# Up projection of a two-stage kernel: the low part of x's last 64 rows in row-half matmuls, and 256 columns everywhere

## The chip, the cores and the metric

The kernel runs on one core of a Trainium2 chip. The metric is the device time of one execution in microseconds; the median of three runs of the kernel before is 454.5 us (454.33 to 455.55).

## What is computed

Two stages. The first is a gated linear attention (an mLSTM cell) over 4 sequences of 768 steps with 8 heads of 40, the second a feed-forward layer on its output x of 3072 tokens by 320:

```python
h = x @ w_in                                                # 320 -> 2048
sp = np.maximum(h, 0.0) + np.log1p(np.exp(-np.abs(h)))
g = h * erf(sp)
return (g @ w_out).astype(np.float32)                       # 2048 -> 320
```

The weights come as float64 and are decoded on the chip.

## The kernel before, in words

The sequence is cut into 12 chunks of 64 steps, so a chunk has 256 tokens. `attention(c)` makes the chunk's attention on TensorE in many small matmuls of 40 or 64 rows: line 509 the scores, 518 the state times the queries, 523 the new state, 531 (536 in the first three chunks) the heads. Line 389 turns the output on TensorE to put features on rows; lines 392 and 393 do this for the last 64 features in the first three chunks, once for either half of 128 rows. Lines 402 and 406 split the turned x into a high part `xh` (rounded to TensorE's short format, fp32r) and the rest `xl`. x has 320 features, so both have three slices of rows: 128, 128, and 64 rows that are there twice, in rows 0 to 63 and again in rows 64 to 127.

w_in is split likewise into `wh` and `wl`, but the 64 rows of its third slice hold both: in `wh[:, 2]` one half of the 128 rows is the high part and the other half the low part, which `weights_tail` arranges (ScalarE line 694 writes the high part to the rows where the decoded word lies, VectorE line 698 the low part to the other half). One matmul with `x[:, 2]`, which is there twice, thus multiplies high and low part of w_in at once.

`mlp(g)` is the feed-forward layer for one chunk k and a quarter q of the 2048 features, 48 blocks in all. Its up projection writes `h` in four groups of 128 features by 256 tokens. For g below 16 (line 759, two steps of 16 matmuls of 256 columns) every group has eight matmuls: three for each full slice (wh x, wh xl, wl x) and two for the third (wh x, wh xl). From g = 16 on (`wide`, four steps of 5 matmuls) x and xl lie side by side as 512 columns, so a group is three matmuls of 512 columns and two of 256, and the sums with x and with xl land in two halves of a PSUM bank. ScalarE copies `h` to `hb` (line 770); for the wide form it copies one half and VectorE adds the other (line 775). `h` has two banks that all steps take in turn. Then come softplus, erf, a product (lines 779 to 787), a split into `gh` and `gl` (797 to 803) and the down projection on TensorE into `pob` (lines 823 to 828, 320 columns), as four steps a block: for each half of the tokens a long one with `gh` and a short one with `gl`.

The order of the work is a list written out in the file, `ORDER`: each entry is a step, and every engine's instructions stand in the order of the steps. Each step has a cost in microseconds beside it that only the search for the list uses.

Of the kernel before, what the change touches and what calls it, by code (L numbers as in the profile page):

```python
# [9 lines left out]
F32 = mybir.dt.float32  # L10
# [23 lines left out]
class Plan:  # L34
# [136 lines left out]
def tile_mlstm_moe(  # L171
# [503 lines left out]
    def weights_tail(i):  # L675
# [4 lines left out]
        def _():  # L680
            raw = new('raw', [128, 1024], R, I32)
            for j in range(2):
                part = 2 * i + j
                nc.sync.dma_start(raw[64 * j:64 * j + 64], w_in.bitcast(I32)[256:320, part * 1024:(part + 1) * 1024])
# [264 lines left out]
```

## Time and profile before

| | |
|---|---|
| median of three runs | 454.5 us |
| profiled execution | 455.36 us |
| its span, first to last instruction | 453.6 us |
| TensorE busy | 441.3 us (97%) |
| VectorE busy | 356.9 us (79%) |
| ScalarE busy | 328.1 us (72%) |
| DMA, HBM traffic | 46.77 MB read, 4.13 MB written |
| TensorE clock granted | 0.999 of full (2.4 GHz) |

Busy shares tell which engine could be the bound; the waits of that engine tell whether it is. Matmuls are pipelined, so the pitch of a run of matmuls is read from the differences of their starts, not from their durations.

### The profile page before, as it was taken

What the parts mean: (1) busy time and instruction counts of PE and PEld (TensorE: products, weight loads), DVE (VectorE), ACT (ScalarE), POOL (GpSimd) and SP (SyncE); (2) the same over time, 40 slices, a digit from 0 to 9 for tenths busy, and PEclk for the clock granted to TensorE, in tenths of its full rate; (3) what the DMA queues carried; (4) which work ended last, traced back from release to release, by engine and by line L of the source; (5) the groups of instructions that cost most, each with busy time, mean ns of one, the idle gap of its engine ahead of it and who ended that gap; (6) DMA issues with size and microseconds to landing.
All of it is one profiled execution on the core that took longest, in us unless ns stands there. A gap on an engine that the chain in (4) does not pass through costs nothing.

```text
span 453.6 us, 13042 instructions
## 1 busy us (share of the span) xinstructions
PE 441.3 (97%) x5542; PEld 396.2 (87%) x5542; DVE 356.9 (79%) x709; ACT 328.1 (72%) x524; POOL 39.0 (9%) x62
## 2 busy tenths in 40 slices
PE   6979999999999999999999999999999999999996
PEld 4558898897999999998998999999998899999996
DVE  4897998799779888877888869978687877665862
ACT  4766999899589987676785777765776476765850
POOL 2000051003111004002001102300000000000000
PEclk9999999999999999999999999999999999999999
DMA  7969797818834053412247114340322100000011
GB/s 257 293 173 335 226 280 223 224 48 259 222 97 127 3 117 106 106 45 87 83 131 206 49 43 124 115 128 1 108 107 85 31 1 0 14 17 17 14 30 29
DMA packets 46826, 51.74 MB, mean 114 GB/s; under 512 B 27056, under 2 KB 31664, under 8 KB 46768
## 3 DMA queue, kind: packets, MB, share of 16 engines
q1 hardware_dynamic: 46768, 50.91, 38.7%
q8 instruction: 43, 0.70, 0.6%
q14 instruction: 15, 0.12, 0.1%
HBM read 46.77 MB, written 4.13 MB: 112 GB/s over the span
## 4 chain that ended last, share of the span: by engine, by line
PE 88%; DVE 6%; DMA 3%; issue 1%; ACT 1%; SPq 1%; DVEq 0%
PE h L759 37%; PE pob L827 11%; PE pob L825 11%; PE pob L828 11%; PE pa L518 3%; PE pa L509 2%; PE pa L531 2%; PE pob L823 2%; PE pa L389 2%; PE pa L523 1%; DMA gd<-x 1%; DMA raw<-in_w_in_dram 1%; PE pob L283 1%; PE pa L446 1%; DVE wo L724 1%
## 5 line engine op out<-in xcount | busy, mean ns | idle before, releaser
L759 PE MATMUL h<-xh,wh 128*128 128x256 f32 (+1 forms) x768 | 203.4, 343 | 1.6 <-DVE xh L406 1.2
L759 PEld LDWEIGHTS h<-xh,wh 128*128 128x128 f32 x768 | 126.3, 188 | 15.6 <-DVE xh L406 1.4
L770 ACT ACTIVATE hb<-h 128x256 f32<-128x256 f32 (+1 forms) x160 | 66.2, 423 | 68.9 <-PE h L759 66.1
L759 PE MATMUL h<-xh,wl 128*128 128x256 f32 x384 | 107.9, 281 | 1.0 <-DVE wl L660 1.0
L827 PE MATMUL pob<-woh,gh 128*128 128x320 f32 x336 | 100.8, 312 | 0.0
L828 PE MATMUL pob<-wo,gh 128*128 128x320 f32 x336 | 99.9, 309 | 0.0
L775 DVE TENSOR_TENSOR hb<-h,hb 128x256 f32<-128x256 f32 x128 | 52.9, 420 | 40.9 <-ACT hb L770 40.0
L759 PEld LDWEIGHTS h<-xh,wl 128*128 128x128 f32 x384 | 72.4, 188 | 2.7 <-DVE wl L660 1.2
L887 ACT ACT_TABLE_LOAD x54 | 69.3, 1283 | 1.7 <-PEq L937 0.8
L787 DVE TENSOR_TENSOR n<-n,hb 128x1024 f32<-128x1024 f32 x48 | 59.0, 1229 | 13.4 <-ACT n L783 13.3
L828 PEld LDWEIGHTS pob<-wo,gh 128*128 128x128 f32 x336 | 63.1, 188 | 1.7
L827 PEld LDWEIGHTS pob<-woh,gh 128*128 128x128 f32 x336 | 63.2, 188 | 0.5
L825 PE MATMUL pob<-woh,gl 128*128 128x320 f32 x336 | 62.3, 311 | 0.0
L487 POOL TENSOR_SCALAR_AFFINE_SELECT dm<-dm 128x512 f32<-128x512 f32 (+1 forms) x40 | 35.6, 892 | 278.2 <-ACT dm L467 275.8
L825 PEld LDWEIGHTS pob<-woh,gl 128*128 128x128 f32 x336 | 53.8, 188 | 2.3
L803 DVE TENSOR_TENSOR gl<-n,gh 128x1024 fp32r<-128x1024 f32 x44 | 53.5, 1222 | 0.3
L779 ACT ACTIVATE n<-hb 128x1024 f32<-128x1024 f32 x48 | 49.5, 1055 | 3.0 <-DVE hb L775 1.7
L783 ACT ACTIVATE n<-n 128x1024 f32<-128x1024 f32 x48 | 50.0, 1055 | 0.2
L797 ACT ACTIVATE gh<-n 128x1024 fp32r<-128x1024 f32 x28 | 29.4, 1054 | 4.1 <-DVE n L787 2.4
L627 DVE TENSOR_TENSOR state<-state,pa 40x328 f32<-40x328 f32 (+1 forms) x36 | 17.8, 494 | 5.0 <-PE pa L531 3.3
L567 DVE TENSOR_TENSOR dm<-pa,dm 128x512 f32<-128x512 f32 x24 | 16.5, 687 | 5.7 <-PE pa L509 5.4
L833 ACT ACTIVATE o<-pob 128x320 f32<-128x320 f32 x22 | 9.4, 434 | 14.9 <-PE pob L825 14.9
(103 smaller groups left out, 481.2 us busy)
## 6 DMA issues: line engine op xcount, KB each, us to landing
qk<-in_qk_dram SPq DMA_DIRECT2D x24, 512.0 KB
kvo<-in_kvo_dram SPq DMA_DIRECT2D x24, 484.0 KB
eT<-gd SPq DMA_DIRECT2D x44, 128.0 KB
raw<-in_w_out_dram SPq DMA_DIRECT2D x16, 320.0 KB
dm<-gd SPq DMA_DIRECT2D x40, 128.0 KB
raw<-in_w_in_dram SPq DMA_DIRECT2D x8, 512.0 KB
out_dram<-o SPq DMA_DIRECT2D x48, 80.0 KB
raw<-in_w_in_dram SPq DMA_DIRECT2D x4, 256.0 KB
```

The source lines that it names most:

```text
L487: nc.gpsimd.affine_select(out=x, in_=x, pattern=[[0, H], [1, L]], compare_op=ALU.is_ge, fill=0.0, base=base, channel_multiplier=-1)
L759: nc.tensor.matmul(h[:, n * T:n * T + n_], w, m, start=(s == 0), stop=(s == len(ops) - 1))
L770: nc.scalar.activation(part(), G(f'h{i}')[:, T:2 * T] if wide else G(f'h{i}'), AF.Copy)
L775: nc.vector.tensor_tensor(part(), G(f'h{i}')[:, 0:T], part(), op=ALU.add)
L779: nc.scalar.activation(new('n0', [128, 1024], ('n0', g)), G('hb'), AF.Softplus)
L783: nc.scalar.activation(G('n0'), G('n0'), AF.Erf)
L787: nc.vector.tensor_tensor(G('n0'), G('n0'), G('hb'), op=ALU.mult)
L803: nc.vector.tensor_tensor(new('gl', [128, 1024], ('gl', g), F32R), G('n0'), G('gh').bitcast(F32), op=ALU.subtract)
L825: nc.tensor.matmul(acc(b), G('gl')[:, ts], woh[:, j], start=False, stop=(j == NFF - 1))
L827: nc.tensor.matmul(acc(b), G('gh')[:, ts], woh[:, j], start=(j == 0), stop=False)
L828: nc.tensor.matmul(acc(b), G('gh')[:, ts], t['wol', j], start=False, stop=False)
L887: plan.run(ORDER, lambda k: nc.scalar.preload_act_table_set(KIND[k]), stay)
```

## The change

From g = 8 on (`TAILS`), the up projection gets a step of its own ahead of the rest: four matmuls of 64 rows by 256 columns, high part of w_in's last 64 rows times `xl`. Two of the four lie on rows 0 to 63 and write bank `h0`, two on rows 64 to 127 and write `h1`, in turn. The product of the two low parts of these rows falls away. The other two steps have 14 matmuls of 256 columns, two groups of seven each, and add to what the new step has begun; the wide form with its addition on VectorE is gone. The blocks below 8 keep two steps of 16.

```diff
-        wide = g >= 16
-        ups = 4 if wide else 2
+        tails = g >= TAILS
+        ends = [('wh', 2, q)]
...
+        if tails:
+            @op('PE', 0.25, mm=4, r=[(('xl', k), b) for b in range(2)] + ends, w=[(('h0', g), 't'), (('h1', g), 't')],
+                tile_=[('h', ('h0', g)), ('h', ('h1', g))], kind='m', name=f'up{g}')
+            def _():
+                h = [new('h', [128, 512], (f'h{i}', g)) for i in range(2)]
+                xr = t['xl', k]
+                for n in range(2):
+                    for i in range(2):
+                        rows, fs = slice(64 * i, 64 * i + 64), slice((4 * q + 2 * i + n) * 128, (4 * q + 2 * i + n + 1) * 128)
+                        nc.tensor.matmul(h[i][:, n * T:(n + 1) * T], wh[rows, 2, fs], xr[rows, 2], start=(n == 0), stop=False)
...
-                    if wide:
-                        ops = [(wh[:, 0, fs], both[:, 0]), (wl[:, 0, fs], x[:, 0]), (wh[:, 1, fs], both[:, 1]),
-                               (wl[:, 1, fs], x[:, 1]), (wh[:, 2, fs], both[:, 2])]
...
+                    ops = [(wh[:, 0, fs], x[:, 0]), (wh[:, 0, fs], xr[:, 0]), (wl[:, 0, fs], x[:, 0]),
+                           (wh[:, 1, fs], x[:, 1]), (wh[:, 1, fs], xr[:, 1]), (wl[:, 1, fs], x[:, 1]),
+                           (wh[:, 2, fs], x[:, 2])] + ([] if tails else [(wh[:, 2, fs], xr[:, 2])])
...
-            if wide:
-                @op('DVE', 0.33, r=[((f'h{i}', g), 0)], w=[(('hb', g), i)])
-                def _(i=i, part=part):
-                    nc.vector.tensor_tensor(part(), G(f'h{i}')[:, 0:T], part(), op=ALU.add)
```

So that the high part lies on rows 0 to 63 for the first two groups of a quarter and on rows 64 to 127 for the other two, `weights_tail` loads and splits in pieces of 256 features instead of 512, two ScalarE and two VectorE instructions where there was one of each; the loads keep their number and bytes, in runs of 2 KB instead of 4.

```diff
-                part = 2 * i + j
-                nc.sync.dma_start(raw[64 * j:64 * j + 64], w_in.bitcast(I32)[256:320, part * 1024:(part + 1) * 1024])
+                nc.sync.dma_start(raw[64 * j:64 * j + 64].rearrange("p (a w) -> p a w", a=2), src[:, :, j])
...
+                for j in range(2):
+                    nc.scalar.activation(wh[rows[j], 2, cs[j]], word(j), AF.Copy)
...
+                for j in range(2):
+                    nc.vector.tensor_tensor(wh[rows[1 - j], 2, cs[j]], word(j), wh.bitcast(F32)[rows[j], 2, cs[j]], op=ALU.subtract)
```

The list `ORDER` is another from entry 340 on. Read against the steps, it places the 40 new steps so: 20 stand between two steps of 128-row matmuls, 19 follow directly on an attention step that ends in 64-row matmuls (scores or heads) and go over to 128-row matmuls, and one follows on 128-row matmuls and is followed by such an attention step. Between the last up step of a block and the new step of the next there is always some down projection or attention.

## Rows read from the trace of the kernel before

**Rows 1.** The page: busy time by engine; TensorE's digits and clock in 40 slices.

```profile
PE 441.3 (97%) x5542; PEld 396.2 (87%) x5542; DVE 356.9 (79%) x709; ACT 328.1 (72%) x524; POOL 39.0 (9%) x62
...
PE   6979999999999999999999999999999999999996
...
PEclk9999999999999999999999999999999999999999
```

**Rows 2.** Waits of TensorE over the run: us in total, times, longest us.

```profile
PE pob L283 <- DVE state L272: 3.5, 1, 3.5
PE h L759 <- DVE xh L406: 1.2, 1, 1.2
PE h L759 <- DVE wl L660: 1.0, 1, 1.0
```

**Rows 3.** The page: the chain that ended last, by engine.

```profile
PE 88%; DVE 6%; DMA 3%; issue 1%; ACT 1%; SPq 1%; DVEq 0%
```

**Rows 4.** Busy time in one stretch: length, then us (count) by engine.

```profile
200.00:220.00 20.00, 20.00 (x210) 18.25 (x209) 15.01 (x33) 13.13 (x23) 2.44 (x2) 1.00 0.25 74
```

**Rows 5.** Pieces of the chain: start us, length us, what.

```profile
63.76 2.11 PE h L759 x16
...
115.79 1.92 PE h L759 x16
...
141.72 3.83 PE h L759 x32
...
168.57 1.87 PE h L759 x10
...
303.59 1.13 PE h L759 x5
...
310.82 0.59 PE pob L825 x4
```

**Rows 6.** Timeline of TensorE around a heads block: start us, length us, what.

```profile
302.23 0.39 PE L759 MATMUL h<-xh,wh 128*128 128x512 f32 x1
302.47 0.28 PE L759 MATMUL h<-xh,wl 128*128 128x256 f32 x1
302.58 0.40 PE L759 MATMUL h<-xh,wh 128*128 128x512 f32 x1
302.92 0.68 PE L531 MATMUL pa<-kvo,dm 64*64 64x41 f32 x32
303.52 0.50 PE L759 MATMUL h<-xh,wh 128*128 128x512 f32 x1
303.86 0.28 PE L759 MATMUL h<-xh,wl 128*128 128x256 f32 x1
```

**Rows 7.** The same block: its first four matmuls, and its last one.

```profile
302.92 0.27 PE L531 MATMUL pa<-kvo,dm 64*64 64x41 f32 x4
...
303.37 0.23 PE L531 MATMUL pa<-kvo,dm 64*64 64x41 f32 x1
```

**Rows 8.** Timeline of TensorE around a column-split transpose of an early chunk.

```profile
46.47 0.27 PE L392 MATMUL pa<-ident,kvo 128*64 128x128 f32 x1
46.67 0.43 PE L393 MATMUL pa<-ident,kvo 128*64 128x128 f32 x2
47.04 0.50 PE L759 MATMUL h<-xh,wh 128*128 128x256 f32 x2
```

**Rows 9.** Groups by line and form: busy us, mean ns, idle before and its releasers.

```profile
L770 ACT ACTIVATE hb<-h 128x256 f32<-128x256 f32 x128 | 47.3, 380 | 65.1 <-PE h L759 62.3 <-issue 2.1 <-ACT hb L770 0.5
L770 ACT ACTIVATE hb<-h 128x512 f32<-128x512 f32 x32 | 18.9, 591 | 3.8 <-PE h L759 3.8
L694 ACT ACTIVATE wh<-raw 64x512 fp32r<-64x512 f32 x4 | 2.7, 670 | 1.6 <-DVE raw L646 1.5
...
L775 DVE TENSOR_TENSOR hb<-h,hb 128x256 f32<-128x256 f32 x128 | 52.9, 420 | 40.9 <-ACT hb L770 40.0
L698 DVE TENSOR_TENSOR wh<-raw,wh 64x512 fp32r<-64x512 f32 x4 | 2.7, 687 | 0.2
```

More of the change, by code (lines that the diff above doesn't have):

```diff
@@ L101 @@
     225, 162, 273, 79, 80, 81, 82, 87, 89, 274, 202, 203, 355, 371, 206, 141, 194, 142, 121, 92, 122, 275, 276, 90, 248,
[64 rows of a table removed]
[53 rows of a table added]
 ]
-PLAIN, JOIN, GH_ACT = 4, 3, 32
+PLAIN, JOIN, GH_ACT, TAILS = 4, 3, 32, 8
 @with_exitstack
@@ L582, in _ @@
                         t[n, c] = x[:, :, i]
-                    t['x', 'both', c] = x
                 heads(r)
@@ L681, in _ @@
             raw = new('raw', [128, 1024], R, I32)
+            src = w_in.bitcast(I32)[256:320, i * 2048:(i + 1) * 2048].rearrange("p (a j w) -> p a j w", a=2, j=2)
             for j in range(2):
-                part = 2 * i + j
-                nc.sync.dma_start(raw[64 * j:64 * j + 64], w_in.bitcast(I32)[256:320, part * 1024:(part + 1) * 1024])
+                nc.sync.dma_start(raw[64 * j:64 * j + 64].rearrange("p (a w) -> p a w", a=2), src[:, :, j])
         decode(R, lambda: pair(t[R]), 512, lambda: pair(t[R])[:, :, 0], ())
-        for j in range(2):
-            part = 2 * i + j
-            cs, here, there = slice(part * 512, (part + 1) * 512), slice(64 * j, 64 * j + 64), slice(64 - 64 * j, 128 - 64 * j)
-            word = lambda here=here: pair(t[R])[here, :, 0].bitcast(F32)
-            @op('ACT', 0.56, r=[(R, 1)], w=[('wt', part)])
-            def _(cs=cs, here=here, word=word):
-                nc.scalar.activation(wh[here, 2, cs], word(), AF.Copy)
-            @op('DVE', 0.62, r=[(R, 1), ('wt', part)], w=[('wh', 2, part)])
-            def _(cs=cs, here=here, there=there, word=word):
-                nc.vector.tensor_tensor(wh[there, 2, cs], word(), wh.bitcast(F32)[here, 2, cs], op=ALU.subtract)
+        for a in range(2):
+            part = 2 * i + a
+            rows = [slice(64 * j, 64 * j + 64) for j in range(2)]
+            cs = [slice(part * 512 + 256 * j, part * 512 + 256 * j + 256) for j in range(2)]
+            word = lambda j, a=a: pair(t[R])[64 * j:64 * j + 64, 256 * a:256 * a + 256, 0].bitcast(F32)
+            @op('ACT', 0.62, r=[(R, 1)], w=[('wt', part)])
+            def _(rows=rows, cs=cs, word=word):
+                for j in range(2):
+                    nc.scalar.activation(wh[rows[j], 2, cs[j]], word(j), AF.Copy)
+            @op('DVE', 0.68, r=[(R, 1), ('wt', part)], w=[('wh', 2, part)])
+            def _(rows=rows, cs=cs, word=word):
+                for j in range(2):
+                    nc.vector.tensor_tensor(wh[rows[1 - j], 2, cs[j]], word(j), wh.bitcast(F32)[rows[j], 2, cs[j]], op=ALU.subtract)
     def weights_out(j):
@@ L734, in acc @@
             return t['po', k][:, 512 * b:512 * b + DM] if k == 1 else pob[b][:, 0:DM]
-        wide = g >= 16
-        ups = 4 if wide else 2
-        whole = [(('hb', g), i) for i in range(ups)]
-        for i in range(ups):
-            @op('PE', 0.937 if wide else 1.915, mm=5 if wide else 16, r=[((n, k), b) for n in ('xh', 'xl') for b in range(2)]
-                + [(n, s, q) for n, s in (('wh', 0), ('wh', 1), ('wh', 2), ('wl', 0), ('wl', 1))],
-                w=[((f'h{i}', g), 0)], tile_=('h', (f'h{i}', g)), kind='m', name=f'up{g}')
+        tails = g >= TAILS
@@ new lines, in mlp @@
+        whole = [(('hb', g), i) for i in range(2)]
+        ends = [('wh', 2, q)]
[9 more added lines that the diff above has]
+                        nc.tensor.matmul(h[i][:, n * T:(n + 1) * T], wh[rows, 2, fs], xr[rows, 2], start=(n == 0), stop=False)
@@ L744, in _ @@
+        for i in range(2):
+            @op('PE', 1.68 if tails else 1.915, mm=14 if tails else 16, r=[((n, k), b) for n in ('xh', 'xl') for b in range(2)] + ends
+                + [(n, s, q) for n, s in (('wh', 0), ('wh', 1), ('wl', 0), ('wl', 1))] + ([((f'h{i}', g), 't')] if tails else []),
+                w=[((f'h{i}', g), 0)], tile_=() if tails else ('h', (f'h{i}', g)), kind='m', name=f'up{g}')
             def _(i=i):
-                h = new('h', [128, 512], (f'h{i}', g))
-                x, xr, both = t['xh', k], t['xl', k], t['x', 'both', k]
@@ L747, in _ @@
-                for n in range(1 if wide else 2):
-                    j = 4 * q + (i if wide else 2 * i + n)
+                h = t[f'h{i}', g] if tails else new('h', [128, 512], (f'h{i}', g))
+                x, xr = t['xh', k], t['xl', k]
+                for n in range(2):
+                    j = 4 * q + 2 * i + n
                     fs = slice(j * 128, (j + 1) * 128)
-                    if wide:
-                        ops = [(wh[:, 0, fs], both[:, 0]), (wl[:, 0, fs], x[:, 0]), (wh[:, 1, fs], both[:, 1]),
-                               (wl[:, 1, fs], x[:, 1]), (wh[:, 2, fs], both[:, 2])]
-                    else:
-                        ops = [(wh[:, 0, fs], x[:, 0]), (wh[:, 0, fs], xr[:, 0]), (wl[:, 0, fs], x[:, 0]),
-                               (wh[:, 1, fs], x[:, 1]), (wh[:, 1, fs], xr[:, 1]), (wl[:, 1, fs], x[:, 1]),
-                               (wh[:, 2, fs], x[:, 2]), (wh[:, 2, fs], xr[:, 2])]
-                    for s, (w, m) in enumerate(ops):
-                        n_ = 2 * T if len(m.shape) == 3 else T
-                        nc.tensor.matmul(h[:, n * T:n * T + n_], w, m, start=(s == 0), stop=(s == len(ops) - 1))
@@ L761, in part @@
-            def part(i=i):
-                n = 1024 // ups
-                return G('hb')[:, i * n:(i + 1) * n]
-            @op('ACT', 0.28 if wide else 0.49, r=[((f'h{i}', g), 0)], w=[(('hb', g), i)],
-                tile_=('hb', ('hb', g)) if i == 0 else ())
-            def _(i=i, part=part):
+                    ops = [(wh[:, 0, fs], x[:, 0]), (wh[:, 0, fs], xr[:, 0]), (wl[:, 0, fs], x[:, 0]),
+                           (wh[:, 1, fs], x[:, 1]), (wh[:, 1, fs], xr[:, 1]), (wl[:, 1, fs], x[:, 1]),
+                           (wh[:, 2, fs], x[:, 2])] + ([] if tails else [(wh[:, 2, fs], xr[:, 2])])
@@ L768, in _ @@
+                    for s, (w, m) in enumerate(ops):
+                        nc.tensor.matmul(h[:, n * T:(n + 1) * T], w, m, start=(s == 0 and not tails), stop=(s == len(ops) - 1 and (n == 1 or not tails)))
+            @op('ACT', 0.49, r=[((f'h{i}', g), 0)], w=[(('hb', g), i)], tile_=('hb', ('hb', g)) if i == 0 else ())
+            def _(i=i):
                 if i == 0:
                     new('hb', [128, 1024], ('hb', g))
-                nc.scalar.activation(part(), G(f'h{i}')[:, T:2 * T] if wide else G(f'h{i}'), AF.Copy)
@@ L772, in mlp @@
-            if wide:
-                @op('DVE', 0.33, r=[((f'h{i}', g), 0)], w=[(('hb', g), i)])
-                def _(i=i, part=part):
-                    nc.vector.tensor_tensor(part(), G(f'h{i}')[:, 0:T], part(), op=ALU.add)
+                nc.scalar.activation(G('hb')[:, i * 512:(i + 1) * 512], G(f'h{i}'), AF.Copy)
         @op('ACT', 0.96, r=whole, w=[(('n0', g), 0)], tile_=('n0', ('n0', g)), table='S')
```

117 rows, old and new, of the table ORDER are left out of this document.

## The prediction

> **What bounds the kernel now.** I read the page's busy shares first: TensorE is busy 441.3 of 453.6 us, and its digits are 9 in every slice from the fourth to the last but one, at full clock throughout [rows 1]. VectorE has 79% and ScalarE 72%, so they are no bound by their sum, but either could still be late at many places. The waits of TensorE decide that: over the whole run the longest wait for another engine is 3.5 us, at the very start, then come 1.2 and 1.0 in the stage that decodes the weights, and nothing else of that size [rows 2]. The chain of waits says the same (88% TensorE), and the stretch from 200 to 220 us shows TensorE at 20.00 of 20 with VectorE at 15.0 and ScalarE at 13.1 [rows 3, 4]. So from about 47 us to the end the time is the sum of TensorE's own work, in the order of the list. What VectorE and ScalarE save is worth nothing; what a matmul step costs or gives counts one to one.
>
> **Two kinds of pitch** are needed, and both are differences of starts, since durations of single matmuls overlap. A run of 128-row up matmuls of 256 columns takes 1.92 us for 16 and 3.83 for 32, so 0.12 each; ten of the wide form, two steps, take 1.87, so 0.935 a step [rows 5]. Second, a change of the array's shape. A 512-column matmul is followed 0.24 us later by the next (302.23 to 302.47), but 0.34 later by the first of the 64-row block of the attention heads: 0.10 of idle array [rows 6]. Leaving is the same: the last small matmul starts at 303.37 and the first full one 0.15 later [rows 6, 7], where the small ones come four at a time in rounds of 0.06 (32 of them from 302.92 to 303.37), so about 0.10 more. Then the first matmul in the new shape waits for its own weights: 303.52 to 303.86 is 0.34 where 0.24 is usual, 0.10 again, because nothing could load them beforehand. The chain gives the sum of the leaving side in one number: 16 up matmuls after a 64-row block take 2.11 against 1.92, five of the wide form take 1.13 against 0.935 [rows 5]. A column-split shape pays it too: the 128x64 transposed tail in the upper half starts 0.20 after its predecessor of 128 columns, and the next full matmul finds the array 0.37 after that pair's start [rows 8].
>
> **Change, part by part.**
>
> Full-array work saved. For the 32 blocks from 16 on, four steps of 0.935 = 3.74 us become 28 matmuls of 0.12, 2 x 14/16 x 1.915 = 3.35: 0.39 saved, 12.5 in all. The eight blocks 8 to 15 go from 3.83 to 3.35: 0.48 each, 3.8. Together 16.3 us. Most of the 0.39 is one 256-column matmul per 128 features; the split into 256 columns gives back a little (a 512 at 0.23 is cheaper than two at 0.12).
>
> The new step of four 64-row matmuls, 40 times. No row shows a 64-row by 128-column matmul, so it is put together. The four of one round of a head block start within 0.02 us of each other, and 32 need 0.45 us of starts: halves of the array do run side by side when they write different banks, which is what h0 and h1 are [rows 7]. So four are two rounds of 0.12 = 0.24. On top, between two full-array steps: 0.10 to enter, 0.10 for the first weights, 0.10 to leave, 0.10 for the first weights after it. 0.64. After or before a block of 64-row matmuls in the list one idle gap and one load are paid anyway, so 0.10 + 0.10 less: 0.44. The list has 20 of either sort: 12.8 + 8.8 = 21.6 us. Bounds of one step: 0.24 from below (the columns must be streamed; less is excluded), 0.88 from above (halves one after the other, 4 x 0.12, with all four gaps; the gaps around the heads block are the nearest rows, hence 0.64 [rows 6]).
>
> What the Trainium skill says bears on the 0.40 of gaps: "TensorEngine Tiling (Array Packing)", Key Properties, has it that a change of tiling mode, not of tile, makes the engine drain. By that rule the step costs what I take; the rows agree for 64x64 and 128x64, and none shows 64x128.
>
> Evacuation. The 128 additions on VectorE (52.9 us) go; ScalarE's copies go from 47.3 + 18.9 to 96 of 0.59 = 57 us [rows 9]. Both lie under TensorE and give nothing.
>
> What is queued behind the new wait. The new step needs both banks of h free, so it waits for the second copy of the block before; on TensorE's queue all later down projections stand behind it. In the list the work between a block's last up matmul and the next new step is never under 0.86 us and in 37 of 39 cases 1.1 or more, counted with 0.59 for a short down step, twice that for a long one and 0.6 or more for an attention step [rows 5, 6]; the copy needs 0.28 for the last matmul's end and 0.59 for itself [rows 6, 9]. So at most a handful of short waits; I take 0, bound 0 to 4 us (eight of 0.5).
>
> Weight tails. Each of four splits becomes two instructions per engine: 0.67 on ScalarE and 0.69 on VectorE now. By the 128-row copies, two of 256 columns cost 2 x 0.38 - 0.59 = 0.17 more, and two additions 2 x 0.42 - 0.69 = 0.15 more [rows 9]. Only in the decode stage, where TensorE waited 1.2 and 1.0 us for such results [rows 2], can this show: bounds 0 and 4 x 0.32 = 1.3; I take 0.2. The four loads on SP's queue keep number and bytes, in pieces half as long; they are covered by the other weights still in flight, and uncovered they could cost no more than the 1.0 above.
>
> The list. It cannot win anything of TensorE's own sum; before, no wait was left in it to remove after 47 us, and the number of 64-row blocks entered from the full shape stays 44. So 0.
>
> Sum: -16.3 + 21.6 + 0.2 = +5.5 us. The profiled execution took 455.36 with a span of 453.6; on it 460.9. It stood 0.86 over the median 454.5, against which I forecast **460.0**.
>
> **Rivals.**
>
> 1, the other side: the shape change is not paid for row halves. The weights of a half are loaded while the full array still streams, and the full array's next weights behind the halves; then a step costs its 0.24, 40 of them 9.6, and the sum is -16.3 + 9.6 + 0.2 = -6.5: 448.0. It decides at (16.3 - 0.2)/40 = 0.40 per step: below that the kernel is faster. For it: inside a shape the next weights are always loaded ahead, and the heads block is split in columns as well as rows [rows 6], which this step is not. Against: every change of shape that the trace has pays. The Trainium skill's "TensorE: Matmul & The Clock Gate", Part 3, The mechanism, says that a load for rows in no conflict is drawn ahead of running matmuls; a full-array matmul holds all rows, so by its own condition this helps only between the halves. Chance 0.20.
>
> 2, partly hidden: one of the two sides (entering or leaving) is free, so all steps cost about 0.44: 17.6 - 16.3 + 0.2 = +1.5, 456.0; with only one gap of 0.10 left, 452. Chance 0.12.
>
> 3, halves one after the other: 0.48 of streaming, 40 x 0.24 more than my sum: 469.6. Against it stands the round of four. Chance 0.08.
>
> 4, the wait for both banks: my sum plus the 4 us: 464. For it: blocks now come as two steps of 1.68 instead of four of 0.94, so ScalarE's copy is later by its length. Chance 0.08.
>
> That the change doesn't do what it says: the time of the streamed columns falls only if the dropped product (low part of w_in's last 64 rows times low part of x) was streamed before; it was, on the other 64 rows of the same 256-column matmul, so that matmul can be halved. No chance is left for that.
>
> **How the numbers follow.** My forecast has 0.52, with 457 to 463 of its own (gaps of 0.08 to 0.12, 0 to 1.3 of decode). A measurement tells 0.3%, 1.4 us, from no change. Faster: rival 1 and a third of rival 2, 0.24. Within 0.3%: most of the rest of rival 2, 0.07. Slower: 0.69. The range goes from rival 1's 448 to rival 4's 464 and leaves out rival 3 and stragglers.
>
> **What would show it.** In the profile after: TensorE still at 20.00 of 20 in the middle; the columns' saving as 28 full matmuls per block at 0.12; the four 64-row matmuls starting in pairs under 0.02 apart, the pairs 0.12 apart; before them a start gap some 0.10 over the usual, after them 0.20 over (0.10 idle and a first matmul with 0.22 to the next instead of 0.12); the additions gone and VectorE under 310 us. Wrong would be: the first 64-row matmul at the ordinary 0.12 behind its predecessor (rival 1), the two of a pair 0.1 apart (rival 3), or waits of TensorE for copies adding to microseconds (rival 4).

## The result and the profile after

The kernel after the change takes 460.6 us (median of four, 459.27 to 462.11) against 454.41 of the kernel before beside it: 1.0139 times as long, 95% interval 1.0096 to 1.0183. Measured once more with the kernels of the second set of experiments it took 461.08 against 455.32, 1.0118 (1.0090 to 1.0146). Forecast were 460.0 and slower.

The page of the kernel after, busy time by engine, TensorE's digits and clock, and the chain by engine and by line:

```profile
PE 444.7 (97%) x5926; PEld 409.4 (90%) x5926; DVE 310.3 (68%) x585; ACT 335.9 (73%) x475; POOL 37.7 (8%) x62
...
PE   6979999999999999999999999999999999999996
...
PEclk9999999999999999999999999999999999999999
...
PE 90%; DMA 4%; DVE 2%; ACT 2%; SPq 1%; issue 1%; POOL 0%; POOLq 0%; DVEq 0%; ACTq 0%
PE h L756 35%; PE pob L814 11%; PE pob L812 11%; PE pob L815 11%; PE h L740 4%; DMA raw<-in_w_in_dram 3%; PE pa L507 3%; PE pa L520 2%; PE pa L498 2%; PE pob L810 2%; PE pa L810 2%; PE pa L378 1%; PE pa L512 1%; PE pob L272 1%; DMA gd<-x 1%; PE pa L812 1%
```

TensorE is as full as before [rows 1, 3], at the same clock, while VectorE lost 46.6 us of work (356.9 to 310.3) that bought nothing. In the chain line 740, the new step, holds 4% of the span, some 17.5 us (40 of 0.44). Its 40 steps in the chain are pieces like the third below (start us, length us, what; around 302 us):

```profile
302.08 0.14 PE pob L815
302.23 0.59 PE pob L812 x4
302.82 0.44 PE h L740 x4
303.26 1.76 PE h L756 x13
```

The timeline of TensorE at the same place shows how the 0.44 comes about. The narrow view of the first pair and of the second cuts the merged group in two:

```profile
302.22 0.60 PE L812 MATMUL pob<-woh,gl 128*128 128x320 f32 x3
302.75 0.39 PE L740 MATMUL h<-xh,wh 64*128 64x256 f32 x2
...
302.98 0.28 PE L740 MATMUL h<-xh,wh 64*128 64x256 f32 x2
303.19 0.39 PE L756 MATMUL h<-xh,wh 128*128 128x256 f32 x1
...
303.53 0.28 PE L756 MATMUL h<-xh,wl 128*128 128x256 f32 x1
303.65 0.28 PE L756 MATMUL h<-xh,wh 128*128 128x256 f32 x1
```

Three matmuls of 320 columns from 302.22 end their turn at 302.66 (three pitches of 0.147); the first pair starts at 302.75, so 0.09 of idle array. The two of a pair start within 0.01 us: merged they last 0.28, as long as the single full matmul at 303.53. From the first pair to the second are 0.23: a load of weights that nothing hides, and a round of streaming. From the second to the first full matmul are 0.21: a round of 0.12 and 0.09 of idle. From there two full matmuls take 0.34 (303.19 to 303.53) where two usually take 0.24 (the next one, 303.53 to 303.65, 0.12): the second load that nothing hides. Together 0.63 us for the step, against 0.64 forecast. Behind a 64-row block one idle gap and one load were paid before the change too [rows 5, 6], and 0.44 are left. The chain has such a step around 308:

```profile
307.98 0.61 PE pa L520 x32
308.59 0.44 PE h L740 x4
309.02 0.78 PE pob L812 x4
```

The down step of four behind it takes 0.78 where 0.59 is usual [rows 5]: the leaving gap and the load, which the kernel before paid behind the 64-row block itself.

One thing stands beside the sum: the span of this execution is only 3.7 us longer than before, 457.3 to 453.6, while the medians differ by 6.2. The start-up, where the two lists are the same, went faster in it: the up step of 16 that starts at 63.76 in the chain before [rows 5], and so ends at 65.87, ends at 64.71 here (chain of the kernel after, from 62 us on):

```profile
62.59 2.11 PE h L756 x16
64.71 2.15 PE pob L810 x8
66.86 0.61 PE pa L507 x32
```

Behind that step, the two executions differ by 4.9 us (3.7 of span and 1.2 of start-up). The start-up varies by as much between executions: the kernel before with 256 columns alone (below), which is the same program up to there, ends this step at 64.82.

### The profile page after: what moved, and what is told of

It reads as the page before. It is cut to its first block, busy times and chain, and to the rows that moved or that the text cites. A ratio compares the mean times of both kernels' runs of the same rounds, so it can differ in the third digit from the quotient of the medians.

```text
span 457.3 us, 13666 instructions
## 1 busy us (share of the span) xinstructions
PE 444.7 (97%) x5926; PEld 409.4 (90%) x5926; DVE 310.3 (68%) x585; ACT 335.9 (73%) x475; POOL 37.7 (8%) x62
## 4 chain that ended last, share of the span: by engine, by line
PE 90%; DMA 4%; DVE 2%; ACT 2%; SPq 1%; issue 1%; POOL 0%; POOLq 0%; DVEq 0%; ACTq 0%
PE h L756 35%; PE pob L814 11%; PE pob L812 11%; PE pob L815 11%; PE h L740 4%; DMA raw<-in_w_in_dram 3%; PE pa L507 3%; PE pa L520 2%; PE pa L498 2%; PE pob L810 2%; PE pa L810 2%; PE pa L378 1%; PE pa L512 1%; PE pob L272 1%; DMA gd<-x 1%; PE pa L812 1%
## 5 line engine op out<-in xcount | busy, mean ns | idle before, releaser
L756 PE MATMUL h<-xh,wh 128*128 128x256 f32 x992 | 180.9, 286 | 0.4 <-ACT wh L644 0.4
L756 PEld LDWEIGHTS h<-xh,wh 128*128 128x128 f32 x992 | 151.1, 188 | 4.9 <-ACT wh L644 0.6
L762 ACT ACTIVATE hb<-h 128x512 f32<-128x512 f32 x96 | 55.6, 591 | 52.5 <-PE h L756 52.1
L790 DVE TENSOR_TENSOR gl<-n,gh 128x1024 fp32r<-128x1024 f32 x44 | 53.2, 1221 | 13.8 <-ACT gh L784 8.3
L476 POOL TENSOR_SCALAR_AFFINE_SELECT dm<-dm 128x512 f32<-128x512 f32 (+1 forms) x40 | 34.3, 868 | 281.1 <-ACT dm L456 224.6
L812 PEld LDWEIGHTS pob<-woh,gl 128*128 128x128 f32 x336 | 51.2, 188 | 1.6
L556 DVE TENSOR_TENSOR dm<-pa,dm 128x512 f32<-128x512 f32 x24 | 16.5, 688 | 22.5 <-PE pa L498 16.1
L740 PE MATMUL h<-xh,wh 64*128 64x256 f32 x160 | 20.1, 329 | 0.0
```

The source lines that it names most:

```text
L476: nc.gpsimd.affine_select(out=x, in_=x, pattern=[[0, H], [1, L]], compare_op=ALU.is_ge, fill=0.0, base=base, channel_multiplier=-1)
L740: nc.tensor.matmul(h[i][:, n * T:(n + 1) * T], wh[rows, 2, fs], xr[rows, 2], start=(n == 0), stop=False)
L756: nc.tensor.matmul(h[:, n * T:(n + 1) * T], w, m, start=(s == 0 and not tails), stop=(s == len(ops) - 1 and (n == 1 or not tails)))
L762: nc.scalar.activation(G('hb')[:, i * 512:(i + 1) * 512], G(f'h{i}'), AF.Copy)
L790: nc.vector.tensor_tensor(new('gl', [128, 1024], ('gl', g), F32R), G('n0'), G('gh').bitcast(F32), op=ALU.subtract)
L812: nc.tensor.matmul(acc(b), G('gl')[:, ts], woh[:, j], start=False, stop=(j == NFF - 1))
```

## Experiments

My theory was the sum of the prediction: what the 64-row step costs is mostly the visit to another shape of the array, 0.40 us whatever it holds. The rivals were a free shape change, halves that don't overlap, the wait for two banks and the new list. Each set of kernels had its own runs of the kernel before; what is compared across sets is the difference to those.

**The kernel after, once more,** for a measure on the chip of the second set.

> The kernel after the change, unchanged, so that it stands on the same chip as the others of this set. My theory and all rivals: 5 to 6 us over the kernel before (459 to 462).

Measured: 461.08 us, 5.8 over the kernel before (interval above). Differences "to the kernel after" below are to these 5.8.

**Two visits in place of one.** The step's two pairs are parted by one full-array matmul, taken from the first up step; number and size of all matmuls stay.

```diff
                         nc.tensor.matmul(h[i][:, n * T:(n + 1) * T], wh[rows, 2, fs], xr[rows, 2], start=(n == 0), stop=False)
+                    if n == 0:
+                        nc.tensor.matmul(h[0][:, 0:T], wh[:, 2, 4 * q * 128:(4 * q + 1) * 128], t['xh', k][:, 2], start=False, stop=False)
...
+                    if tails and i == 0 and n == 0:
+                        del ops[6]
```

> The kernel after the change with the step's two pairs parted by one full-array matmul, which is taken from the first up step: the same matmuls in number and size, but two visits to the 64-row shape in place of one. My theory: one more visit costs two idle gaps of 0.10 and two loads of 0.10 that nothing covers, 40 x 0.40 = 16 us, 476.6 us (473 to 479). Rival, shape change free: 460.6, no difference. Rival, only one side is paid: 40 x 0.20 = 8 us, 468.6.

Measured: 474.62 us, 19.6 over the kernel before (1.0426, 1.0377 to 1.0475), so 13.8 more than the kernel after. The timeline of TensorE around one step:

```profile
317.84 0.68 PE L520 MATMUL pa<-kvo,dm 64*64 64x41 f32 x32
318.45 0.38 PE L740 MATMUL h<-xh,wh 64*128 64x256 f32 x2
318.76 0.38 PE L742 MATMUL h<-xh,wh 128*128 128x256 f32 x1
319.07 0.38 PE L740 MATMUL h<-xh,wh 64*128 64x256 f32 x2
319.39 0.56 PE L816 MATMUL pob<-woh,gl 128*128 128x320 f32 x2
```

Every start is 0.31 behind the one before, 318.45 to 319.39: a round of 0.12, an idle gap of 0.09 and a load of 0.10, again and again, also for the one full matmul in between. Same arithmetic, 13.8 us more, 0.35 for each of 40 visits; the timeline has 0.38 (0.94 from the first pair to what follows, less the full matmul's 0.12 and the 0.44 of a single visit). Free shape changes (no difference) and changes paid on one side (8 us) are out.

**One pair left out.** Only the first pair of each step stays; the product with x's low part is missing for half of the features in blocks 8 to 47.

```diff
-                for n in range(2):
+                for n in range(1):
```

> The kernel after the change with only the first pair of the four 64-row matmuls (the product with x's low part is missing for half of the features in blocks 8 to 47). My theory, 0.40 us a visit whatever it holds and 0.12 a round: 40 x 0.12 = 4.8 us less than the kernel after the change, 456. Rival, the cost goes with the matmuls and not with the visit: half of the step's 21.6 us, 450.

Measured: 455.82 us, 0.55 over the kernel before (1.0011, 0.9988 to 1.0034), so 5.2 less than the kernel after: 0.13 a round. Half the work of the step gave back a quarter of its price by the sum (21.6), or 0.30 of the 17.2 that leaving it out gave (below); the visit kept the rest. The timeline has the pair at 264.27 and the full matmul 0.31 later:

```profile
264.27 0.38 PE L740 MATMUL h<-xh,wh 64*128 64x256 f32 x2
264.58 0.51 PE L756 MATMUL h<-xh,wh 128*128 128x256 f32 x2
264.93 0.28 PE L756 MATMUL h<-xh,wl 128*128 128x256 f32 x1
```

**All four on one half.** The same four matmuls, all on rows 0 to 63; for the second two groups of a quarter these rows hold the low part of w_in, so that the product there is another one.

```diff
-                        rows, fs = slice(64 * i, 64 * i + 64), slice((4 * q + 2 * i + n) * 128, (4 * q + 2 * i + n + 1) * 128)
+                        rows, fs = slice(0, 64), slice((4 * q + 2 * i + n) * 128, (4 * q + 2 * i + n + 1) * 128)
```

> The kernel after the change with all four 64-row matmuls on rows 0 to 63 (for the second two groups of a quarter these rows hold the low part of w_in, so that part of the output is another product), same number, size, banks and one visit. My theory, that the two row halves really stream side by side, whatever their place in the list: on one half there are four rounds of 0.11 in place of two, 40 x 0.22 = 8.8 us slower than the kernel after the change, 469.8. Rival, halves never overlapped and the step always held four rounds: no difference, 461.

Measured: 468.73 us, 13.5 over the kernel before (1.0291, 1.0255 to 1.0327), 7.7 over the kernel after, where 8.8 were expected. The timeline of one step, which ends 0.67 after its start, against 0.44 with two halves:

```profile
312.73 0.68 PE L520 MATMUL pa<-kvo,dm 64*64 64x41 f32 x32
313.33 0.73 PE L740 MATMUL h<-xh,wh 64*128 64x256 f32 x4
314.00 0.71 PE L812 MATMUL pob<-woh,gl 128*128 128x320 f32 x3
```

So the two halves do stream side by side, and the pairs' starts are no mere queue entries.

**The pairs broken up in program order.** Both matmuls of rows 0 to 63 first, then both of rows 64 to 127.

```diff
-                for n in range(2):
-                    for i in range(2):
+                for i in range(2):
+                    for n in range(2):
```

> The kernel after the change with the four 64-row matmuls in another order: both of rows 0 to 63 first, then both of rows 64 to 127. My theory, that two row halves run side by side when they follow each other: only the second and third now overlap, so three rounds in place of two, 40 x 0.11 = 4.4 to 4.8 us slower than the kernel after the change (465). Rival, halves of the array don't overlap at all and the pairs' starts in the trace are only queue entries: no difference.

Measured: 460.25 us, 4.9 over the kernel before (1.0115, 1.0083 to 1.0148): no different from the kernel after. My expectation failed, and by its number the rival would be right; but the run on one half rules that rival out. The narrow views of one step:

```profile
270.12 0.39 PE L740 MATMUL h<-xh,wh 64*128 64x256 f32 x2
...
270.35 0.28 PE L740 MATMUL h<-xh,wh 64*128 64x256 f32 x2
270.56 0.39 PE L756 MATMUL h<-xh,wh 128*128 128x256 f32 x1
```

They start in pairs, 0.23 apart, and leave 0.21 later, to the hundredth like the ordinary order. Two matmuls of one half can't do that: on one half the step took 0.67. So the third of the program, the first of the other half, started beside the first, ahead of the second. That the four came to TensorE in the new order is borne out by the trace: in all 40 steps the second start is 0.006 to 0.007 behind the first, where the ordinary order has 0.002 to 0.004.

The Trainium skill ("TensorE: Matmul & The Clock Gate", Part 3, The mechanism) has it that matmuls start and end strictly in program order. The measurement differs here for the starts: between the two halves of the rows they do not keep the program's order. The ends are modelled in the profile, so it says nothing of them.

**Four full-array matmuls in the step's place,** with its claim of both banks, and **the same product folded into the up steps,** eight matmuls a group, without a step. Both have the product of the two low parts again. The second diff shows only the line with the product; the step's body and its claim of the banks go as in the last diff of this section.

```diff
-                        rows, fs = slice(64 * i, 64 * i + 64), slice((4 * q + 2 * i + n) * 128, (4 * q + 2 * i + n + 1) * 128)
+                        rows, fs = slice(0, 128), slice((4 * q + 2 * i + n) * 128, (4 * q + 2 * i + n + 1) * 128)
```

```diff
...
-                           (wh[:, 2, fs], x[:, 2])] + ([] if tails else [(wh[:, 2, fs], xr[:, 2])])
+                           (wh[:, 2, fs], x[:, 2])] + [(wh[:, 2, fs], xr[:, 2])]
...
```

> The kernel after the change with the step kept where it is and with its claim of both banks, but its four matmuls on all 128 rows (so the product of the two low parts is there again). My theory: 4 x 0.12 = 0.48 us and no change of shape, 19.2 in place of 21.6, 458.2 us (457 to 460), the same as with the matmuls folded into the up steps. Rival, the wait for both banks costs: as slow as the change or slower (460.6 and above) while the folded form is faster by the wait. Rival, shape change free: 470.2.

> The kernel after the change without the step of 64-row matmuls: each group of features gets its eighth full-array matmul of 256 columns back, inside the two up steps (as blocks 0 to 7 have it), so no change of shape and no claim of both banks at once; list and all else as after the change. My theory: 40 x 0.48 = 19.2 us in place of 21.6, 458.2 us (457 to 460), slightly faster than the change. Rival, shape change free: 40 x (0.48 - 0.24) = 9.6 us slower than the change, 470.2. Rival, the wait for both banks costs microseconds: below 455.

Measured: 458.87 us in the step's place, 3.8 over the kernel before (1.0085, 1.0055 to 1.0116), and 459.24 folded, 4.2 over (1.0080, 1.0053 to 1.0108). The two are the same within the noise, which is some 2 us, so the claim of both banks costs nothing that can be seen, and the median of each is lower than that of the kernel after (5.8 to 6.2 over before), though the intervals overlap: 2.4 us were expected, 1.6 to 2.4 came out. The timeline of the first shows the step without a visit:

```profile
302.44 0.76 PE L812 MATMUL pob<-woh,gl 128*128 128x320 f32 x4
303.03 0.63 PE L740 MATMUL h<-xh,wh 128*128 128x256 f32 x4
303.50 0.40 PE L756 MATMUL h<-xh,wh 128*128 128x256 f32 x2
303.74 0.29 PE L756 MATMUL h<-xh,wl 128*128 128x256 f32 x1
```

303.03 is four pitches of 0.147 after 302.44, with no gap; the next full matmul comes 0.47 later and its successors at the usual 0.24 for two. Twice the streaming, and cheaper than the visit between full-array matmuls (0.63); behind a 64-row block, where the step costs 0.44, it is not.

**256 columns alone.** The kernel before, each 512-column matmul of the wide form issued as two of 256.

```diff
-                        n_ = 2 * T if len(m.shape) == 3 else T
-                        nc.tensor.matmul(h[:, n * T:n * T + n_], w, m, start=(s == 0), stop=(s == len(ops) - 1))
+                        if len(m.shape) == 3:
+                            for z in range(2):
+                                nc.tensor.matmul(h[:, z * T:(z + 1) * T], w, m[:, z], start=(s == 0 and z == 0), stop=(s == len(ops) - 1 and z == 1))
+                        else:
+                            nc.tensor.matmul(h[:, n * T:(n + 1) * T], w, m, start=(s == 0), stop=(s == len(ops) - 1))
```

> The kernel before, with each 512-column matmul of the wide up projection issued as two of 256 columns (eight matmuls a group in place of five, same sums, same additions, same list). My theory, from the pitches: 0.96 in place of 0.935 us a group, 128 x 0.025 = 3 us slower than before, 457.5. Rival, the weight loads (eight in place of five) are not hidden under 256 columns: 3 x 0.1 us x 128 = 38 us slower. Rival, 256 and 512 columns cost the same per column: no difference.

Measured: 457.97 us, 2.65 over the kernel before (1.0054, 1.0032 to 1.0077). This half of the change costs by itself what the pitches say, and the folded kernel, which has the same matmuls under the new list and without the additions on VectorE, is not faster for being rid of them.

**The split of the weight tails alone,** in the kernel before (the diff of `weights_tail` in The change, nothing else).

> The kernel before, with only the new loading and splitting of w_in's last 64 rows (pieces of 256 features, two instructions where there was one); its up projection reads either layout alike. My theory: 0 to 1.3 us slower than before, most likely 0.2, so the same within what can be measured (454.5). Rival, the decode stage sets the start and the longer splits are paid in full with the shorter loads: 2 us or more.

Measured: 455.45 us against 455.32 (1.0004, 0.9985 to 1.0024). Nothing, although each pair of instructions takes 0.86 on ScalarE and 0.93 on VectorE in place of 0.67 and 0.69; groups by line of the kernel after:

```profile
L689 DVE TENSOR_TENSOR wh<-raw,wh 64x256 fp32r<-64x256 f32 x8 | 3.7, 466 | 0.2
...
L684 ACT ACTIVATE wh<-raw 64x256 fp32r<-64x256 f32 x8 | 3.4, 430 | 0.5 <-DVE raw L634 0.4
```

**The step left out,** its product missing.

```diff
-                h = [new('h', [128, 512], (f'h{i}', g)) for i in range(2)]
-                xr = t['xl', k]
...
+                pass
...
-                h = t[f'h{i}', g] if tails else new('h', [128, 512], (f'h{i}', g))
+                h = new('h', [128, 512], (f'h{i}', g))
...
```

> The kernel after the change with the four 64-row matmuls left out (the product of w_in's last 64 rows with the low part of x is missing in blocks 8 to 47), the step empty, nothing else moved. My theory (a step costs 0.64 us between full-array steps and 0.44 us next to a 64-row block): 21.6 us less than the change, 460.6 - 21.6 = 439.0 us, between 437 and 441. Rival, the shape change is free (0.24 us a step): 9.6 us less, 451.0. Rival, the changed list is what made it slower and the step costs what the search put down for it (0.25 us): 10 us less, 450.6.

Measured: 443.65 us, 11.4 under the kernel before (0.9744, 0.9700 to 0.9787), so 17.2 less than the kernel after, where 21.6 were expected. The rivals' 9.6 and 10 are out, but 4.4 us are missing. The waits of TensorE in this kernel (us in total, times, longest us):

```profile
PE pob L272 <- DVE state L261: 3.5, 1, 3.5
PE h L751 <- DVE xh L395: 1.9, 1, 1.9
PE h L751 <- issue: 1.5, 1, 1.5
PE pa L507 <- DVE qe L469: 1.1, 1, 1.1
...
PE pa L507 <- ACT hb L757: 0.9, 1, 0.9
...
PE pa L512 <- DVE vg L486: 0.5, 1, 0.5
```

The whole view adds to 13.5 us here and to 8.3 in the kernel after. The 5.2 between them are of the size of what is missing: with TensorE's work cut by 5%, VectorE and ScalarE are late where they had been in time. A single execution of each and a start-up that varies by a microsecond make that a fit, not a proof. Two numbers on record point the same way. TensorE's busy time in this kernel is 20.5 us under the kernel after, close to the 21.6:

```profile
PE 424.2 (96%) x5766; PEld 397.1 (90%) x5766; DVE 310.1 (70%) x585; ACT 335.5 (76%) x475; POOL 39.7 (9%) x62
```

And the folded kernel, with the same list and measured beside this one, has 160 full-array matmuls more, 19.2 us at 0.12, but takes only 15.6 us more (459.24 to 443.65). Between these two there is no visit, and 3.6 us are missing all the same. So the gap lies, in the main, with the kernel without the product and not with the price of a visit.

## Why the prediction was right, point by point

**The bound** was TensorE's own work, and stayed it: 46.6 us less on VectorE gave nothing [rows 1]. ScalarE's copies went from 66.2 to 55.6 us, with 57 forecast [rows 9], but ScalarE as a whole rose, 328.1 to 335.9: the new list loads its function tables 65 times instead of 54, 1.28 us each, for which the prediction had not looked. In the profile after, it shows in TensorE's waits at one place alone, around 120 us (below). VectorE came to 310.3, with "under 310" forecast.

**The columns saved.** The up steps of 14 take 1.67 to 1.68 in the chain after, two of them 3.55 behind a change of shape, as against 1.92 and 3.83 of 16 [rows 5]:

```profile
106.43 1.67 PE h L756 x14
...
132.24 3.55 PE h L756 x28
...
182.39 3.35 PE h L756 x28
```

3.55 less the 0.20 for idle and load is 3.35, the figure of the sum, and where a down step stands between the new step and the two, 3.35 is what the chain has. The price of 256 columns in it was measured alone, 2.65 against 3.

**The step:** 0.63 and 0.44 against 0.64 and 0.44, put together from a block of another shape [rows 6, 7] and each part then found by itself: 0.09 to 0.10 idle on entering and on leaving, 0.10 to 0.11 for a load on either side, 0.12 a round. One sign was put wrong: the pairs were to start 0.12 apart and start 0.23 apart, since the first pair waits for its own load, which the sum counts and the list of signs leaves out. By experiment the visits are worth 13.8 us of 16, the round 5.2 of 4.8. The rule of the Trainium skill that stood beside it ("TensorEngine Tiling (Array Packing)", Key Properties: a change of mode drains the engine) agrees with the timeline of the 64x128 shape as well.

**Costed at nothing or little.** The wait for both banks: nothing seen (458.87 with it, 459.24 without). The tails' split: 0.13, inside the noise. The list was taken as 0, and here the prediction was off by 0.6 to 0.8 us: around 120 us TensorE waits for ScalarE or VectorE under the new list, where under the old one no wait worth naming stood behind 47 us. It waits 0.8 us in both profiles of the kernel after, 0.7 with four full matmuls and 0.6 folded. The chain of the kernel after passes there through ScalarE, with one of the function-table loads (L874):

```profile
117.50 0.60 PE pa L812 x4
118.12 0.44 ACT o L820
118.58 1.28 ACT L874
119.87 1.07 ACT n L766
120.94 0.66 PE pa L507 x31
```

Whether the list costs more than that stays open: folded, it stood 4.2 over before, where 256 columns under the old list stood 2.65, and the intervals of the two overlap.

**What the experiments leave open in the sum.** The step and the saving were measured apart in one run only, the one without the step. It stood 11.4 under before, where the sum without the step has 16.1, and 17.2 under after, where it has 21.6. Both are short by 4.4 to 4.7, and they cancel in the forecast. If that were the true size of both terms, the good agreement of the total would be luck. The timelines, the busy times and the folded kernel speak against it, as said at that run; how much of the shortfall is waits is not shown.

**Rivals.** Free shape change (448.0): refuted by two visits. One side paid: refuted by the timeline, which has both gaps and both loads. Halves one after the other (469.6): that kernel was in effect built, with all four on one half, and took 468.7; the change is not that. The wait for both banks (464): refuted as above.

As it is built here, in 40 blocks and with 256 columns everywhere, the step can't beat the kernel before by these prices: all 40 at their cheapest place would cost 17.6 against the 16.3 saved. In a block that was wide it saves 0.39 us and costs 0.44 there; it would pay, by 0.05, only if one visit beside a 64-row block served two blocks ((2 x 0.24 + 0.20) / 2 = 0.34), which takes four banks at a time where `h` has two. A form that keeps the 512-column matmuls of the two full slices and halves only the third would save some 0.45 a block (an estimate: four times the 0.23 of 512 columns less the 0.12 of 256), no more than break even beside a 64-row block. Neither was tried.

## What to carry to other kernels

A matmul on half the rows costs what it streams plus a visit: 0.40 us here between full-array matmuls, 0.20 beside work that has left the full shape anyway. So halving matmuls of 256 columns pays only where enough of them come together in one visit; four of them saved 0.24 us of streaming and paid 0.40. Price a change of shape from the starts around one that the trace already has, entering gap, first load, leaving gap, first load after, and add it per visit, not per matmul.

## What was not expected of the hardware

Matmuls on different halves of the rows pass one another: with both of one half ahead of both of the other in the program, pairs still start 0.01 us apart and the step still takes 0.44 us, where four on one half take 0.67. So here the order in which they were written did not matter.

Between full-array matmuls, four full matmuls of 128 rows, 0.47 us, were cheaper than four of half the rows, 0.63.
